# Gated layer of an attention block: PSUM copies of a finished chunk one step later and on ACT alone; scaling of the last weights on ACT, their mean and rests on DVE

## The chip, the cores and the metric

The kernel runs on one core of a Trainium2 chip. The metric is the device time of one execution in microseconds (us). Before the change it is 907.14 us, the median of three runs (907.09, 907.14 and 909.45). Engines are named as in the profile: PE (TensorE matmul), PEld (its weight loads), ACT (ScalarE), DVE (VectorE), POOL (GpSimd) and SP (SyncE, which only issues DMAs here).

## The reference, cut to what matters

Attention with a bias by relative position (4 batches, 8 heads, 576 tokens, heads of 64) gives x with 2304 rows and 512 columns. Then come two layers, all in float32:

```python
# gated layer: x 2304x512; w1, w2 512x1024; w3 1024x1024; w_out 1024x512
a = x @ w1
b = x @ w2
x2 = (a * b @ w3) @ w_out
# last layer: w_in 512x1024, wo2 1024x512, g_ln 1024
h = x2 @ w_in
e = np.exp(h - np.max(h, axis=-1, keepdims=True))
solu = h * e / (np.sum(e, axis=-1, keepdims=True) + 1e-09)
mu = np.mean(solu, axis=-1, keepdims=True)
var = np.mean((solu - mu) ** 2, axis=-1, keepdims=True)
out = (solu - mu) / np.sqrt(var + 1e-06) * g_ln @ wo2
```

The kernel folds `w3 @ w_out` into one matrix on the chip. It scales each row of `wo2` by `g_ln`, and takes the mean over the 1024 scaled rows off each of them, so that `mu` needs no subtraction later.

## The kernel before

**Precision by pairs.** PE multiplies fp32r operands. Each float32 operand is held as a rounded part (hi, an ACT copy) and the rest (lo, a subtraction on DVE or POOL), and each product is three matmuls, hi·hi, hi·lo and lo·hi (`three`, lines 76 to 81). `split` (line 59) makes such a pair: the ACT copy is line 61, the subtraction is line 62, on POOL unless an engine is given.

**Weights arrive as 64-bit words.** They are turned into float32 by a chain of five instructions (`f64_steps`, lines 69 to 73): an absolute value on ACT (line 69), then four on DVE (70 to 73). A conversion is a Python generator (`f64`, line 572). It yields after each instruction, and its last part is `then`, which may give back a `rest` to be run one yield later. A list of waiting conversions is worked off by `convert(n)` (line 607): it steps the two oldest in turn until n yields that did something are counted. A yield of "wait" and the end of a generator count nothing.

**Steps of the gated layer** (`Gated.run`, line 984). The tokens form 6 chunks of 384; with 8 slices of the 1024 middle columns that makes 48 pairs (c, f). Step s issues: the stores of the chunks finished before (`put_outs`); the product a·b of step s-1 (`gate`: ACT copy line 767, DVE product line 768, to HBM by an ACT DMA, line 803); `stage1` of step s (24 matmuls, `ab<-x,ab`); the splits of the slices that are multiplied in this step (`split_g`, lines 61 and 62, `gh` and `gl`); loads of later slices; `convert(3)`, `convert(1)`; `stage2` for one or two slices (12 matmuls each, `x<-gh,wf` and `x<-gl,wf`), which sum over f in one PSUM tile of 4 banks; the sums and splits of a later chunk's input (`next_x`, lines 722, 727 and 729); and `convert(4)`. All engines work in order, so this order of issue decides what stands behind what.

**End of a chunk.** When `stage2` has done f = 7, `x2_out` (line 787) copies the 4 banks to SBUF right there, two on ACT and two on DVE in turn (line 796, tile `x2s`), and the next step stores them. The PSUM tile has one buffer, so the first `stage2` of the next chunk needs it empty.

**Last weights.** After the fold the list holds 8 conversions of `w_in`, 8 of `wo2` (`cv_wo2`, line 886), the mean (`mean_rows`, line 906), 8 last steps of `wo2` (`out_wo2`, line 926), 7 mixtures of `w_in` (`mixed`) and the first input of the last layer. `cv_wo2` scales the tile on POOL (line 895), stores it to `gw_d`, and adds it to `mean` on POOL (lines 898 and 900). `mean_rows` splits `mean`, and after 8 yields multiplies it with a tile of 1/1024 on PE (line 922) and copies the result with ACT (line 923). `out_wo2` loads each scaled tile again, subtracts the mean on DVE (line 934) and splits it with the rest on POOL. The last two of these wait until the last chunk's `stage1` has begun, at step 40.

Of the kernel before, what the change touches and what calls it, by code (L numbers as in the profile page):

```python
# [7 lines left out]
F = mybir.dt.float32  # L8
# [4 lines left out]
ALU = mybir.AluOpType  # L13
# [10 lines left out]
TC = 384  # L24
# [12 lines left out]
class Chip:  # L37


    def __init__(self, tc):  # L40
        self.tc, self.nc = tc, tc.nc
# [478 lines left out]
class Gated:  # L520
# [11 lines left out]
    def __init__(self, ch, i, x_d, x2_d, gw_d, g_d):  # L532
        self.ch, self.nc, self.i = ch, ch.nc, i
        self.x_d, self.x2_d, self.gw_d, self.g_d = x_d, x2_d, gw_d, g_d
        self.left, self.tail, self.right, self.psl, self.psr = (contextlib.ExitStack() for _ in range(5))
        self.M, self.freed = {}, 0
        self.AB, self.W3, self.X, self.XS, self.PS, self.G, self.WF, self.XP = ({} for _ in range(8))
        self.W = [None] * 8
        self.place, self.XC = {}, {}
        self.queue, self.active, self.turn, self.done, self.outs, self.count = [], [], 0, set(), [], 0  # L540
# [246 lines left out]
    def x2_out(self, c):  # L787
        for o in range(0, 4, 2):
            if self.W[0]:
                t = [self.rp.tile([128, 512], F, tag="cm", name="x2s", bufs=6) for _ in range(2)]  # L790
            else:
                t = self.rp.tile([128, 2, 512], F, tag="w3", name="x2s", bufs=3)
                t = [t[:, 0], t[:, 1]]
            for q in range(2):
                copy = self.nc.vector.tensor_copy if q else self.nc.scalar.copy
                copy(t[q][:, :TC], self.XP[c][:, o + q, :TC])
                r = (o + q) * 128
                self.outs.append((self.x2_d[c][r : r + 128], t[q][:, :TC]))

# [86 lines left out]
    def cv_wo2(self, f):  # L886

        nc = self.nc
        if f == 0:
            self.gl = self.pp.tile([128, 8], F, name="gl", tag="gl")  # L890
            self.ch.load(self.gl, self.i["gln"])
            self.mean = self.pp.tile([128, 512], F, name="mean", tag="mean")

        def then(x):
            nc.gpsimd.tensor_scalar(out=x, in0=x, scalar1=self.gl[:, f : f + 1], scalar2=1.0, op0=ALU.mult, op1=ALU.mult)  # L895
            self.ch.load(self.gw_d[f * 128 : f * 128 + 128], x)
            if f == 0:
                nc.gpsimd.tensor_scalar(out=self.mean, in0=x, scalar1=1.0, scalar2=1.0, op0=ALU.mult, op1=ALU.mult)
            else:
                nc.gpsimd.tensor_tensor(out=self.mean, in0=self.mean, in1=x, op=ALU.add)  # L900
            self.done.add(("wo2", f))

        src = self.i["wo2"].bitcast(U)[f * 128 : f * 128 + 128].rearrange("p (a b) -> p a b", a=1)
        return self.f64(src, 1, then, lambda: f == 0 or ("wo2", f - 1) in self.done)

    def mean_rows(self):

        nc = self.nc
        yield
        while not self.done.issuperset([("wo2", n) for n in range(8)]):  # L910
            yield "wait"
        onef = self.rp.tile([128, 512], F, tag="cm", name="onef", bufs=6)
        nc.gpsimd.memset(onef[:, :128], 1.0 / FF)
        ones = self.rp.tile([128, 512], R, tag="cm", name="ones", bufs=6)[:, :128]
        nc.scalar.copy(ones, onef[:, :128])
        t = self.rp.tile([128, 2, 512], R, tag="w3", name="tmp", bufs=3)
        self.ch.split(t[:, 0], t[:, 1], self.mean)
        for _ in range(8):
            yield
        ps = self.aps.tile([128, 2, 512], F, tag="ab", name="ab")[:, 0]  # L920
        for x in range(2):
            nc.tensor.matmul(ps, ones, t[:, x], start=x == 0, stop=x == 1)
        nc.scalar.copy(self.mean, ps)
        self.done.add("mean")

    def out_wo2(self, f):
        yield
        while "mean" not in self.done or (f == 6 and self.last) or (f == 7 and not self.W[6]):
            yield "wait"
        x = self.rp.tile([128, 512], F, tag="cm", name="cm", bufs=6)  # L930
        self.ch.load(x, self.gw_d[f * 128 : f * 128 + 128])
        yield
        yield
        self.nc.vector.tensor_tensor(out=x, in0=x, in1=self.mean, op=ALU.subtract)
        if f < 3:
            t = self.rp.tile([128, 2, 512], R, tag="w3", name="w3", bufs=3)
        elif f < 6:
            t = self.rp.tile([128, 2, 512], R, tag="raw", name="raw", bufs=4)
        elif f == 6:
            self.spare = self.place[0].tile([128, 2, 2, 512], R, tag="ab0", name="ab0")  # L940
        if f > 5:
            t = self.spare[:, f - 6]
        self.ch.split(t[:, 0], t[:, 1], x)
        self.W[f] = t

    def early(self, n):
# [37 lines left out]
    def run(self):  # L984
        steps = [(c, f) for c in range(NC) for f in range(8)]

        order = sorted(steps, key=lambda g: g if g[0] > 1 else (0, g[1] // 2 if g[1] < 2 else g[1], g))
        at = {g: s for s, g in enumerate(order)}
        late = [(self.cv_win, u) for u in range(8)] + [(self.cv_wo2, f) for f in range(8)]
        late += [(self.mean_rows,)] + [(self.out_wo2, f) for f in range(8)]  # L990
        late += [(self.mixed, i) for i in range(7)] + [(self.first_pair,)]
        self.last = True
        plan, n, loaded, used = {}, 0, 0, 0
        for s in range(2 * len(steps)):
            many = 0 if s < self.LAG else 1 if s < self.LAG + 8 else 2
            plan[s] = [g for g in steps[n : n + many] if at[g] < s - self.NEAR]
            n += len(plan[s])
        for s in range(len(self.EARLY), len(steps) + self.NEAR + 1):
            m = s - self.FLAG
            fold = 0 <= m < 8  # L1000
            pace = 4 if s < len(steps) else 2
            now = order[s] if s < len(steps) else None
            self.put_outs()
            for key in list(self.PS):
                self.gate(*key)
            if now:
                self.stage1(*now)
                self.last = now[0] + 1 < NC
                self.freed = 0 if self.last else now[1] + 1
            for g in plan[s]:  # L1010
                self.split_g(*g)
            while s > self.LAG - 3 and loaded < min(used + 4, len(steps)) and at[steps[loaded]] < s - 1:
                self.load_g(*steps[loaded])
                loaded += 1
            used += len(plan[s])
            if fold:
                ps = self.fold(m)
            many = 6 if fold else pace if plan[s] else 7
            self.convert(3)
            self.put_stores()  # L1020
            self.convert(many - 3)
            if fold:
                if now:
                    self.gate(*now)
                self.folded(m, ps)
                self.convert(6)
                if m == 7:
                    self.queue += late
                    self.feed()
            for g in plan[s]:  # L1030
                self.stage2(*g)
                if g[1] == 7:
                    self.x2_out(g[0])
            if now and s > 7 and now[0] + 1 < NC:
                self.next_x(max(2, now[0] + 1), s % 8)
            if plan[s] and not fold:
                self.convert(pace)
        self.put_stores()
        while self.queue or self.active:
            self.convert(1)  # L1040
        self.put_outs()
# [289 lines left out]
```

## Time and profile before

| | |
|---|---|
| median of three runs | 907.14 us |
| the profiled execution's own time | 905.76 us |
| its span, first to last instruction | 904.0 us |
| PE busy | 857.2 us, 95% of the span |
| DVE, ACT, POOL busy | 642.8, 497.0, 348.0 us |
| mean granted TensorE clock | 0.989 |

A span is the time from the first to the last instruction; what lies around it is 1.76 us here. A row of a timeline gives the start, the duration and the engine of an instruction, and in square brackets how long its engine was idle before it and which instruction ended that. The steps that the change touches run from 500 to 692 us; the last layer begins at 692 us.

### The profile page before, as it was taken

Reading aid. Unit: us, or ns where it says so; the run is one execution under the profiler, and the core shown is the slowest. Engines: PE = TensorE matmul, PEld = TensorE weight load, DVE = VectorE, ACT = ScalarE, POOL = GpSimd, SP = SyncE. Lnnn points to the kernel's source line nnn. Section 1 sums busy time; section 2 is a strip of 40 time slices with the busy share of each in tenths; the row PEclk is TensorE's granted clock in tenths of the full one; section 3 lists DMA queues with packets and bytes.
Section 4 is the critical chain, followed back from the end, with each engine's and each line's share of the span. In section 5 each row is a group of like instructions: output and inputs, shape, how many; then the busy total and the mean of one; then the engine's idle time right before and its main releaser. Section 6 shows DMA issues by size and latency. Waiting matters only on the chain.

```text
span 904.0 us, 16035 instructions
## 1 busy us (share of the span) xinstructions
PE 857.2 (95%) x5430; PEld 772.6 (85%) x5430; DVE 642.8 (71%) x1505; ACT 497.0 (55%) x1052; POOL 348.0 (38%) x412
## 2 busy tenths in 40 slices
PE   7979999999999789889999998989999899999998
PEld 3549999999999679878988998989998688888886
DVE  8988989999999789887752677562444855555552
ACT  7978989999999745443322324232334544444432
POOL 3038988888887640000000013340434433323300
PEclk9998999999999999999999999999999999999999
DMA  6897897897985566664523586643234011111001
GB/s 229 295 313 187 232 247 201 256 255 209 294 225 135 190 207 207 240 203 154 190 81 128 180 272 209 221 132 117 70 120 143 1 46 47 48 47 47 24 23 47
DMA packets 93490, 146.31 MB, mean 162 GB/s; under 512 B 11744, under 2 KB 58208, under 8 KB 93408
## 3 DMA queue, kind: packets, MB, share of 16 engines
q1 hardware_dynamic: 86496, 135.85, 49.0%
q10 hardware_dynamic: 6912, 9.44, 2.9%
q8 instruction: 43, 0.70, 0.3%
q14 instruction: 39, 0.32, 0.1%
HBM read 81.93 MB, written 41.30 MB: 136 GB/s over the span
## 4 chain that ended last, share of the span: by engine, by line
PE 72%; DVE 10%; DMA 9%; ACT 3%; issue 3%; POOL 2%; SPq 1%; ACTq 0%; DVEq 0%; POOLq 0%
PE op L446 7%; PE sp L363 6%; PE ab L79 6%; PE ab L80 6%; PE ab L81 6%; PE tp L403 6%; PE o L80 4%; PE o L79 4%; PE o L81 4%; PE ps L191 3%; PE x L80 3%; PE x L81 3%; PE x L79 3%; DMA k<-kr 2%; PE hx L79 2%
## 5 line engine op out<-in xcount | busy, mean ns | idle before, releaser
L79 PE MATMUL ab<-x,ab 128*128 128x384 f32 x320 | 108.4, 339 | 3.0 <-DVE a L768 2.3
L80 PE MATMUL ab<-x,ab 128*128 128x384 f32 x320 | 107.8, 337 | 0.1
L81 PE MATMUL ab<-x,ab 128*128 128x384 f32 x320 | 107.7, 337 | 0.0
L491 DVE TENSOR_TENSOR etl<-tp,eth 128x512 fp32r<-128x512 f32 (+1 forms) x160 | 99.4, 629 | 10.8 <-ACT eth L477 8.4
L393 POOL TENSOR_SCALAR e<-e,st 128x576 f32<-128x576 f32 x128 | 95.1, 754 | 29.8 <-DVE st L389 26.8
L381 ACT ACTIVATE e<-e,st 128x576 f32<-128x576 f32 x128 | 100.2, 783 | 6.0 <-DVE st L374 6.0
L374 DVE CUSTOM_DVE_ANT_0 e<-sp,bt 128x576 f32<-128x576 f32 x128 | 95.5, 747 | 4.1 <-PE sp L363 2.3
L477 ACT CAST eth<-tp 128x512 fp32r<-128x512 f32 (+1 forms) x160 | 85.3, 543 | 18.6 <-PE tp L403 11.9
L403 PE MATMUL tp<-idt,e 128*128 128x128 f32 x576 | 88.0, 276 | 5.5 <-DVE ell L491 3.0
L895 POOL TENSOR_SCALAR cm<-cm,gl 128x512 f32<-128x512 f32 x8 | 6.7, 842 | 219.8 <-DVE cm L73 219.8
L363 PE MATMUL sp<-k,q 128*128 128x288 f32 x256 | 73.5, 302 | 8.6 <-DVE st L374 6.1
L403 PEld LDWEIGHTS tp<-idt,e 128*128 128x128 f32 x576 | 70.2, 142 | 7.7 <-DVE ell L491 3.2
L363 PE MATMUL sp<-k,qz 128*128 128x288 f32 x256 | 72.5, 298 | 0.0
L80 PE MATMUL x<-gl,wf 128*128 128x384 f32 x192 | 65.3, 340 | 5.7 <-DVE gl L62 5.5
L446 PE MATMUL op<-eth,v 128*128 128x288 f32 x256 | 66.0, 339 | 0.4 <-ACT o L479 0.4
L79 PE MATMUL x<-gh,wf 128*128 128x384 f32 x192 | 64.6, 336 | 0.6 <-ACT gh L61 0.6
L81 PE MATMUL x<-gh,wf 128*128 128x384 f32 x192 | 64.5, 336 | 0.0
L79 PEld LDWEIGHTS ab<-x,ab 128*128 128x128 f32 x320 | 60.4, 189 | 4.7 <-DVE a L768 3.7
L80 PEld LDWEIGHTS ab<-x,ab 128*128 128x128 f32 x320 | 60.4, 189 | 0.4 <-DVE x L729 0.4
L1153 POOL TENSOR_TENSOR st<-st,half 128x1 f32<-128x1 f32 x18 | 9.9, 553 | 132.0 <-DVE st L1152 132.0
L81 PEld LDWEIGHTS ab<-x,ab 128*128 128x128 f32 x320 | 60.4, 189 | 0.0
L363 PEld LDWEIGHTS sp<-k,q 128*128 128x128 f32 x256 | 48.8, 191 | 10.6 <-DVE st L374 7.0
(211 smaller groups left out, 2354.3 us busy)
## 6 DMA issues: line engine op xcount, KB each, us to landing
bias_d<-rs SPq DMA_DIRECT2D x36, 295.5 KB, 4.0
qkr<-in_qk SPq DMA_DIRECT2D x16, 640.0 KB, 5.6
k<-kr SPq DMA_DIRECT2D x64, 144.0 KB, 5.7
x_d<-o SPq DMA_DIRECT2D x64, 144.0 KB, 4.2
g_d<-a ACTq DMA_DIRECT2D x48, 192.0 KB, 2.5
gl<-g_d SPq DMA_DIRECT2D x48, 192.0 KB, 2.6
q<-qh SPq DMA_DIRECT2D x64, 128.0 KB, 3.0
raw<-in_wo SPq DMA_DIRECT2D x16, 512.0 KB, 5.0
```

The source lines that it names most:

```text
L79: mm(out, a[0], b[0], start=first, stop=False, skip_group_check=more)
L80: mm(out, a[0], b[1], start=False, stop=False, skip_group_check=more)
L81: mm(out, a[1], b[0], start=False, stop=last, skip_group_check=more)
L191: nc.tensor.matmul(ps[32 * q : 32 * q + 32, x:y], self.cf, m, start=True, stop=True, tile_position=(0, 32 * q))
L363: nc.tensor.matmul(ps[:, half, :HS], w[("q", "qz")[x]][:, h, q * 128 : q * 128 + 128], w["k"][:, h, half * HS : half * HS + HS], start=x = ...
L374: self.nc.vector.tensor_tensor_reduce(out=halves(e), in0=ps[:, :, :HS], in1=halves(self.BT[(self.pairs[n][0], k)]), scale=-0.125, scalar=3e38,
L381: self.nc.scalar.activation(e, e, AF.Exp, bias=st[:, c : c + 1], scale=-1.0, accum_out=st[:, 2 + 2 * c : 3 + 2 * c])
L393: self.nc.gpsimd.tensor_scalar(out=e, in0=e, scalar1=st[:, c : c + 1], scalar2=1.0, op0=ALU.mult, op1=ALU.mult)
L403: tr = lambda c, src: nc.tensor.transpose(ps[: src.shape[1], c * 128 : c * 128 + 128], src, self.idt)
L446: nc.tensor.matmul(w["op"][:, half, :HS], lhs, rhs, start=c == 0 and x == 0, stop=c == 4 and x == 1)
L477: self.nc.scalar.copy(hi, src)
L491: self.nc.vector.tensor_tensor(out=lo, in0=src, in1=hi.bitcast(F), op=ALU.subtract)
```

## The change

Three things change. `x2_out` is no longer called at the end of `stage2`: the chunk is put on a list, `full`, and copied in the next step, behind `gate`, `stage1` and `split_g` and ahead of the loads and conversions (after the last step, behind `put_stores`). All four copies are on ACT. In `cv_wo2` the scaling is an ACT multiplication, the first sum an ACT copy, and the other sums DVE additions, one yield later. In `mean_rows` and `out_wo2` the rests are DVE subtractions, in `out_wo2` one yield later.

```diff
--- before.py
+++ after.py
@@ -533,6 +533,7 @@
         self.ch, self.nc, self.i = ch, ch.nc, i
         self.x_d, self.x2_d, self.gw_d, self.g_d = x_d, x2_d, gw_d, g_d
         self.left, self.tail, self.right, self.psl, self.psr = (contextlib.ExitStack() for _ in range(5))
+        self.full = []
         self.M, self.freed = {}, 0
         self.AB, self.W3, self.X, self.XS, self.PS, self.G, self.WF, self.XP = ({} for _ in range(8))
         self.W = [None] * 8
@@ -792,8 +793,7 @@
                 t = self.rp.tile([128, 2, 512], F, tag="w3", name="x2s", bufs=3)
                 t = [t[:, 0], t[:, 1]]
             for q in range(2):
-                copy = self.nc.vector.tensor_copy if q else self.nc.scalar.copy
-                copy(t[q][:, :TC], self.XP[c][:, o + q, :TC])
+                self.nc.scalar.copy(t[q][:, :TC], self.XP[c][:, o + q, :TC])
                 r = (o + q) * 128
                 self.outs.append((self.x2_d[c][r : r + 128], t[q][:, :TC]))
 
@@ -892,13 +892,18 @@
             self.mean = self.pp.tile([128, 512], F, name="mean", tag="mean")
 
         def then(x):
-            nc.gpsimd.tensor_scalar(out=x, in0=x, scalar1=self.gl[:, f : f + 1], scalar2=1.0, op0=ALU.mult, op1=ALU.mult)
+            nc.scalar.mul(x, x, self.gl[:, f : f + 1])
             self.ch.load(self.gw_d[f * 128 : f * 128 + 128], x)
             if f == 0:
-                nc.gpsimd.tensor_scalar(out=self.mean, in0=x, scalar1=1.0, scalar2=1.0, op0=ALU.mult, op1=ALU.mult)
-            else:
-                nc.gpsimd.tensor_tensor(out=self.mean, in0=self.mean, in1=x, op=ALU.add)
-            self.done.add(("wo2", f))
+                nc.scalar.copy(self.mean, x)
+                self.done.add(("wo2", f))
+                return
+
+            def rest():
+                nc.vector.tensor_tensor(out=self.mean, in0=self.mean, in1=x, op=ALU.add)
+                self.done.add(("wo2", f))
+
+            return rest
 
         src = self.i["wo2"].bitcast(U)[f * 128 : f * 128 + 128].rearrange("p (a b) -> p a b", a=1)
         return self.f64(src, 1, then, lambda: f == 0 or ("wo2", f - 1) in self.done)
@@ -914,7 +919,7 @@
         ones = self.rp.tile([128, 512], R, tag="cm", name="ones", bufs=6)[:, :128]
         nc.scalar.copy(ones, onef[:, :128])
         t = self.rp.tile([128, 2, 512], R, tag="w3", name="tmp", bufs=3)
-        self.ch.split(t[:, 0], t[:, 1], self.mean)
+        self.ch.split(t[:, 0], t[:, 1], self.mean, nc.vector)
         for _ in range(8):
             yield
         ps = self.aps.tile([128, 2, 512], F, tag="ab", name="ab")[:, 0]
@@ -940,7 +945,9 @@
             self.spare = self.place[0].tile([128, 2, 2, 512], R, tag="ab0", name="ab0")
         if f > 5:
             t = self.spare[:, f - 6]
-        self.ch.split(t[:, 0], t[:, 1], x)
+        self.nc.scalar.copy(t[:, 0], x)
+        yield
+        self.nc.vector.tensor_tensor(out=t[:, 1], in0=x, in1=t[:, 0].bitcast(F), op=ALU.subtract)
         self.W[f] = t
 
     def early(self, n):
@@ -1009,6 +1016,8 @@
                 self.freed = 0 if self.last else now[1] + 1
             for g in plan[s]:
                 self.split_g(*g)
+            while self.full:
+                self.x2_out(self.full.pop())
             while s > self.LAG - 3 and loaded < min(used + 4, len(steps)) and at[steps[loaded]] < s - 1:
                 self.load_g(*steps[loaded])
                 loaded += 1
@@ -1030,12 +1039,14 @@
             for g in plan[s]:
                 self.stage2(*g)
                 if g[1] == 7:
-                    self.x2_out(g[0])
+                    self.full.append(g[0])
             if now and s > 7 and now[0] + 1 < NC:
                 self.next_x(max(2, now[0] + 1), s % 8)
             if plan[s] and not fold:
                 self.convert(pace)
         self.put_stores()
+        while self.full:
+            self.x2_out(self.full.pop())
         while self.queue or self.active:
             self.convert(1)
         self.put_outs()
```

## Rows read from the trace of the kernel before

**Rows 1.** Busy time by stretch: PE, PEld, DVE, ACT, POOL, granted clock, DMA share, GB/s

```profile
500.00:692.00 192.00, 185.72 (x1055) 182.81 (x1054) 109.86 (x172) 60.60 (x129) 55.16 (x48) 1.00 0.49 161
538.00:600.00 62.00, 56.98 (x323) 55.68 (x322) 44.10 (x62) 20.91 (x43) 28.43 (x24) 1.00 0.64 205
600.00:632.00 32.00, 31.96 (x184) 31.64 (x183) 8.84 (x18) 6.01 (x14) 0.00 (x0) 1.00 0.35 115
```

**Rows 2.** Waits of PE, 500 to 692 us: total, times, longest

```profile
PE x L80 <- DVE gl L62: 5.5, 6, 2.6
PE x L79 <- ACT gh L61: 0.6, 1, 0.6
```

**Rows 3.** Timeline of PE, the matmuls that waited most

```profile
516.81 0.44 PE L80 MATMUL x<-gl,wf 128*128 128x384 f32 x1 [0.73 <-DVE gl L62]
...
552.10 0.44 PE L80 MATMUL x<-gl,wf 128*128 128x384 f32 x1 [1.66 <-DVE gl L62]
...
561.14 0.44 PE L79 MATMUL x<-gh,wf 128*128 128x384 f32 x1 [0.60 <-ACT gh L61]
561.77 0.44 PE L80 MATMUL x<-gl,wf 128*128 128x384 f32 x1 [0.19 <-DVE gl L62]
...
598.40 0.44 PE L80 MATMUL x<-gl,wf 128*128 128x384 f32 x1 [2.57 <-DVE gl L62]
```

**Rows 4.** Timeline around the end of chunk 1, 545 to 551 us

```profile
545.93 0.34 PE L79 MATMUL ab<-x,ab 128*128 128x384 f32 x1
...
546.13 0.48 ACT L796 COPY x2s<-x 128x384 f32<-128x384 f32 x1 [7.47 <-PE x L81]
...
546.64 0.56 DVE L796 COPY x2s<-x 128x384 f32<-128x384 f32 x1 [6.68 <-ACT x2s L796]
...
547.23 0.48 ACT L796 COPY x2s<-x 128x384 f32<-128x384 f32 x1 [0.62 <-DVE x2s L796]
...
547.61 0.93 ACT L727 CAST x<-xs 128x384 fp32r<-128x384 f32 x2
...
550.10 0.34 PE L79 MATMUL x<-gh,wf 128*128 128x384 f32 x1
```

**Rows 5.** The chain of waits, 540 to 570 us: start, us, what

```profile
547.74 0.56 DVE x2s L796
...
554.42 6.14 DMA gl<-g_d
```

**Rows 6.** The chain of waits, 570 to 605 us

```profile
586.70 6.99 DVE cm L934 x6
593.70 1.13 DVE xs L722
```

**Rows 7.** Groups of DVE, 538 to 600 us: busy us, mean ns, idle before

```profile
L62 DVE TENSOR_TENSOR gl<-gl,gh 128x384 fp32r<-128x384 f32 x14 | 10.6, 798 | 0.2 <-ACT gh L61 0.2
L934 DVE TENSOR_TENSOR cm<-cm,mean 128x512 f32<-128x512 f32 x6 | 7.0, 1232 | 0.0
...
L722 DVE TENSOR_TENSOR xs<-x 128x384 f32<-128x384 f32 x2 | 3.2, 1636 | 0.0
```

**Rows 8.** Groups of POOL, 538 to 640 us

```profile
L900 POOL TENSOR_TENSOR mean<-mean,cm 128x512 f32<-128x512 f32 x7 | 9.8, 1403 | 0.6
...
L62 POOL TENSOR_TENSOR w<-cm,w 128x512 fp32r<-128x512 f32 x3 | 5.0, 1698 | 10.9 <-ACT w L61 10.9
```

**Rows 9.** Line 934, whole span: duration ns least, median, most

```profile
L934 DVE TENSOR_TENSOR cm<-cm,mean x8: 683/693/1781, 586.7 to 632.2; 128x512 f32<-128x512 f32 x8
```

**Rows 10.** Groups of ACT, 500 to 692 us

```profile
L69 ACT ACTIVATE cm<-raw 128x512 f32<-128x512 f32 x8 | 5.4, 671 | 7.5 <-DMA raw<-in_wo 7.5
...
L61 ACT CAST w<-cm 128x512 fp32r<-128x512 f32 x3 | 1.8, 623 | 1.4 <-DVE cm L934 1.4
```

**Rows 11.** Timeline of ACT, two waits that hold what stands behind

```profile
560.58 0.99 ACT L61 CAST gh<-gl 128x384 fp32r<-128x384 f32 x2 [3.24 <-DMA gl<-g_d]
...
579.05 0.59 ACT L923 COPY mean<-ab 128x512 f32<-128x512 f32 x1 [2.03 <-PE ab L922]
```

## The prediction, on record before the run

> **What bounds the kernel now.** I read the busy time by stretch first. From 500 to 692 us, all of the gated layer that the change can reach, PE is busy 185.72 of 192.00 us at a granted clock of 1.00, so PE sets the pace and only its 6.28 idle us can be won [rows 1]. None of the three things changed takes a matmul away or adds one. DVE (109.86 us), ACT (60.60 us) and POOL (55.16 us) are far from full on average [rows 1], so their busy time by itself is worth nothing; what counts is when they deliver.
>
> The waits of PE come next. All 6.1 us of them are for the split of a slice, `gl` or `gh`, at the head of `stage2` [rows 2]. The timeline shows where: 0.73 us at 516.81, 1.66 at 552.10, 0.60 and 0.19 just after 561, 2.57 at 598.40, together 5.75 us [rows 3]. The first three places are the first `stage2` of a chunk, or the step after one.
>
> Then the timeline and the chain around one chunk end say why. ACT had reached the copy of the x2 tile 7.47 us early, stood at it until PE finished, and DVE stood 6.68 us behind it [rows 4]. In these microseconds both could have done the conversions and the next `gate` and splits that are queued behind. They start only when the last copy is over: ACT and DVE take turns, each waiting for the other, from 546.13 to 547.74 + 0.56 = 548.30 [rows 4, 5], 2.17 us. PE needs only 550.10 - 545.93 = 4.17 us for `stage1` [rows 4] and then wants a split that has four conversions, a gate and these copies before it. The 0.79 us after 561 come from the same delay: the load of that `gl` was issued only at 554.42 and took 6.14 us to land [rows 5], and ACT waited 3.24 us for it [rows 11].
>
> The 2.57 us have a second cause. Behind the copies of chunk 2, six subtractions of the mean take 6.99 us in a row [rows 6], 1.232 us each, where the least of that line is 0.683 and the median 0.693 [rows 7, 9]. In the same stretch POOL runs the rests of these tiles at 1.698 us each [rows 8], and the two `xs` sums behind take 1.636 us each [rows 7]. DVE is slowed while POOL works on its own tiles. A sum of 384 columns can't need more than the 0.693 us of 512, so this one queue loses 6 x (1.232 - 0.693) + 2 x (1.636 - 0.693) = 5.1 us.
>
> **The change part by part.**
>
> *The copies, one step later.* Now `gate` and `split_g` of the next step stand before the copies, on ACT and on DVE. What still stands behind the copies is the conversions of that step. Take T as PE's end of the chunk. ACT comes to its four copies before T and waits; then they take 3 x 0.38 + 0.48 = 1.62 us, by the distance of two starts (547.23 to 547.61) and one duration [rows 4]. PE is in `stage1` until T + 4.17, so the PSUM tile is empty 2.55 us before the next chunk's `stage2` wants it. The conversions released at T + 1.62 have until the next `stage2` but one, at T + 4.17 + 4.17 + 4.17 = T + 12.5 (two slices are 24 matmuls, as `stage1` is), for a step's work of DVE, which is 44.10/62.00 of 8.3 us = 5.9 us [rows 1]. It fits by 5 us. The stores of x2 and the loads behind them on SP go out one step later too, but SP no longer stands at a store whose copy waits for PE. So the waits of 0.73, 1.66 and 0.79 us go: 3.18 us. What is late next would be a slice's load, with two steps in hand.
>
> *All copies on ACT.* ACT takes 12 x 0.48 = 5.8 us more, DVE 12 x 0.56 = 6.7 us less [rows 4, 5]. Four in a row on ACT are 0.55 us shorter than the four taken in turn. On this the Trainium skill ("TensorEngine Tiling (Array Packing)", PSUM Bottleneck) says the opposite: use both ScalarE and VectorE to empty PSUM. Two engines side by side would need some 1.04 us by these rows, so ACT alone would be 0.58 us later; but the trace shows turns, not two side by side, and either figure lies under the 4.17 us of `stage1`, so the rule would take something only where ACT comes late, which is the third rival below.
>
> *Scaling and sums of wo2.* POOL loses seven sums of 1.403 us and eight scalings [rows 8]. ACT gets eight scalings and one copy. The trace has no ACT multiplication by a column from SBUF; the nearest rows are an absolute value of the same tile at 0.671 and a cast at 0.623 us [rows 10], and I take 0.67: 8 x 0.67 + 0.62 = 6.0 us on an engine that is busy 20.91 of 62.00 us [rows 1]. DVE gets seven sums at 0.693 us [rows 9], 4.9 us. A new wait comes with it: ACT's scaling waits for DVE's last conversion step, and the `gate` and split copies queue behind it on ACT, for which DVE then waits. That is bounded by zero (DVE has other work at hand) and by 0.67 + 0.48 = 1.15 us a scaling; with 2.4 us free in a step of 8.3 I take zero on PE. SP's store of the scaled tile waits for ACT in place of POOL; same queue, same place.
>
> *Rests of the mean and of out_wo2.* Nine more DVE subtractions at 0.693 us [rows 9], 6.2 us, and nine less on POOL, of 1.698 us each in the first three [rows 8]. In exchange DVE works undisturbed. Over 538 to 632 us: 52.9 us busy now [rows 1], less six copies (3.4), plus fourteen sums and rests (9.7; two rests come after), less 5.1 and at least 14 x (0.798 - 0.693) = 1.5 us of slowing on the splits [rows 7]: 52.6 of 94 us. The 2.57 us wait at 598.40 goes: its queue had 5.1 us of slowing and 2.17 of copies in it and gets up to six rests (4.2) back, spread over more steps.
>
> *More yields.* Eight in `cv_wo2`, eight in `out_wo2`: 16 at 8 a step are two steps, 17 us. Six `out_wo2` would end near 594 + 17 = 611 us instead of at 594 [rows 6]. The last two wait for step 40 anyway, and DVE is busy only 8.84 us of the 32 from 600 to 632 [rows 1]: covered. The matmuls of `mean_rows` move a step too. ACT's copy of their result waits for PE (2.03 us now [rows 11]), and where it falls behind a `stage2` it holds the next gate as the x2 copies did. Bounds: nothing, or another 2.57 us; I take 0.75, near the least chunk-end wait, as only one copy and not four stands there.
>
> *The sum.* 3.18 + 2.57 - 0.75 = 5.0 us off a span of 904.0: 899.0. The profiled execution took 905.76, so 1.76 us around it gives 900.8. The median before, 907.14, is 1.38 above that execution; on its footing the forecast is 902.1 us.
>
> **The rivals.**
>
> 1. *The stall at 598 stays.* DVE, with the rests on it, hands over the splits late, or the mean's copy on ACT takes the place of the x2 copies. For: six subtractions and six rests are 12 x 0.693 = 8.3 us, a whole step. Against: three yields each spread them over more than two steps. Then only the 3.18 us at the chunk ends are won: 907.14 - 3.2 = 903.9.
>
> 2. *The gain is given back.* PE comes earlier, and loads of `gl` (6.14 us once [rows 5]) or the last layer's first splits end last instead. For: the DMA share is 0.64 from 538 to 600 us [rows 1]. Against: it is 0.35 from 600 to 632, where PE is busy 31.96 of 32.00 [rows 1]. Gain near 0.6: 906.5.
>
> 3. *ACT frees the PSUM tile late.* Alone, and behind `gate` and a split that waits for its load (3.24 us [rows 11]), it ends at 3.24 + 1.62 = 4.86, 0.7 us after PE wants the tile, at five chunk ends: 3.5 of the 5.0 us gone, 905.6.
>
> 4. *Slower: ACT and DVE in lockstep.* Each of the eight scalings holds ACT until DVE's step is done and then DVE for 1.15 us, 9.2 us in all, and PE waits it out. It decides once DVE's work in a step is above 8.3 - 1.15 = 7.1 us; it is 5.9 on average, more where two conversions meet. 907.14 - 5.0 + 9.2 = 911.3.
>
> **How the numbers follow.** Forecast 0.64; rivals 0.12, 0.09, 0.06 and 0.09. The forecast's own range is 900.2 (every idle us of PE but 0.3 won, and nothing added: 907.14 - 6.0 = 901.1, and 0.9 for the scatter of runs) to 904.0. To hold 0.8 the range goes on through the first rival and most of the two next: 900.2 to 906.3. A measurement here tells 0.3%, 2.7 us, from no change, so faster means below 904.4: the forecast (0.62 of its 0.64) and most of rival 1 (0.10) give 0.72; no change takes the rest of these and rivals 2 and 3, 0.19; slower 0.09.
>
> **What would show it.** Right: the x2 copies are four on ACT a step after the chunk's end, within 1.7 us, with PE in `ab` matmuls; PE's waits for `gl` from 500 to 692 us add up to about 1 us instead of 6.1; the lines 72, 62, 722 and 934 on DVE keep to one duration up to 630 us; POOL is empty until the mixtures. Wrong: a PE wait of over 1 us behind the mean's copy (rival 1), behind an x2 copy (3), ACT's scaling named as what DVE waits for (4), or the layer ending 5 us earlier with the last layer as much longer (2).

## The result, and the profile after

The changed kernel takes 897.62 us (median of 6 runs, 897.14 to 902.96), the one before 907.12 us in the same comparison. The ratio is 0.9906, with a 95% interval of [0.9885, 0.9927]: 9.5 us faster, 6.6 to 10.4. The forecast was 902.1 us with a range of 900.2 to 906.3. The direction was right, and so was the main mechanism, the place of the copies. The gain is nearly twice the forecast, and the time lies below the range. The profiled execution took 898.74 us, with a span of 897.0. Of the runs further down, one of six of the changed kernel took 1685.01 us, and the median there is that of the other five.

The busy time by stretch answers to [rows 1], with the same columns:

```profile
500.00:692.00 192.00, 191.53 (x1088) 189.07 (x1087) 104.26 (x185) 74.94 (x161) 26.22 (x26) 1.00 0.52 171
538.00:600.00 62.00, 62.00 (x358) 61.90 (x358) 38.23 (x72) 26.48 (x55) 0.21 (x1) 1.00 0.66 218
600.00:632.00 32.00, 32.00 (x186) 32.00 (x185) 9.76 (x18) 9.52 (x21) 0.00 (x0) 1.00 0.32 103
```

PE is never idle from 538 to 632 us. Of the waits in [rows 2] this is all that is left from 500 to 690 us:

```profile
PE x L80 <- DVE gl L62: 0.2, 1, 0.2
```

The end of chunk 1 on the timeline, to be held against [rows 4]:

```profile
545.30 0.34 PE L79 MATMUL ab<-x,ab 128*128 128x384 f32 x1
...
545.50 0.48 ACT L796 COPY x2s<-x 128x384 f32<-128x384 f32 x1 [1.71 <-PE x L81]
...
545.87 1.25 ACT L796 COPY x2s<-x 128x384 f32<-128x384 f32 x3
...
547.55 0.74 ACT L895 ACTIVATE cm<-cm,gl 128x512 f32<-128x512 f32 x1
...
549.46 0.34 PE L79 MATMUL x<-gh,wf 128*128 128x384 f32 x1
```

ACT comes 1.71 us early instead of 7.47. The four copies last from 545.50 to 547.12, 1.62 us as forecast, and PE comes for the tile at 549.46, 2.3 us after it is free. The groups of DVE from 538 to 600 us, for [rows 7], and two groups of ACT from 500 to 692 us:

```profile
L62 DVE TENSOR_TENSOR gl<-gl,gh 128x384 fp32r<-128x384 f32 x14 | 7.1, 549 | 0.0
L903 DVE TENSOR_TENSOR mean<-mean,cm 128x512 f32<-128x512 f32 x7 | 4.8, 685 | 0.1
...
L939 DVE TENSOR_TENSOR cm<-cm,mean 128x512 f32<-128x512 f32 x6 | 4.0, 686 | 0.6 <-DMA cm<-gw_d 0.6
```

```profile
L895 ACT ACTIVATE cm<-cm,gl 128x512 f32<-128x512 f32 x8 | 5.8, 727 | 7.2 <-DVE cm L73 7.2
...
L928 ACT COPY mean<-ab 128x512 f32<-128x512 f32 x1 | 0.6, 589 | 3.1 <-PE ab L927 3.1
```

With POOL empty, DVE's splits fall from 798 to 549 ns and its subtractions of the mean from 1232 to 686. ACT waits 7.2 us for DVE ahead of the eight scalings and 3.1 us for the mean's product, and neither reaches PE.

**How much of it lies in the changed steps.** The matmuls are the same 5430 in both kernels, so PE's own marks can be compared: the first `x` matmul after 503 us, ahead of the first wait that changed, and the first `hx` matmul of the last layer. In the profile of before they start at 503.22 and 691.80, 188.57 us apart; in the one after at 503.60 and 684.77, 181.18 apart. That is 7.39 us, where the idle time of the waits that went is 5.75 [rows 3]. So two questions were open: where the other 1.6 us come from, and where the 2.1 us between this profile and the medians come from. Most experiments below give this distance, called the stretch.

### The profile page after: what moved, and what is told of

Same layout as the page of the kernel before. It is cut to its first block, busy times and chain, and to the rows that moved or that the text cites. A ratio compares the mean times of both kernels' runs of the same rounds, so it can differ in the third digit from the quotient of the medians.

```text
span 897.0 us, 15995 instructions
## 1 busy us (share of the span) xinstructions
PE 855.3 (95%) x5430; PEld 773.3 (86%) x5430; DVE 633.8 (71%) x1509; ACT 506.5 (56%) x1073; POOL 317.6 (35%) x387
## 4 chain that ended last, share of the span: by engine, by line
PE 71%; DVE 8%; DMA 7%; issue 2%; ACT 2%; POOL 2%; SPq 1%; POOLq 0%; ACTq 0%; DVEq 0%
PE op L446 7%; PE ab L80 7%; PE ab L79 7%; PE ab L81 7%; PE sp L363 6%; PE tp L403 6%; PE o L80 4%; PE o L79 4%; PE o L81 4%; PE x L80 3%; PE x L81 3%; PE x L79 3%; DMA k<-kr 2%; PE t L1174 2%; PE hx L79 2%
## 5 line engine op out<-in xcount | busy, mean ns | idle before, releaser
L769 DVE TENSOR_TENSOR a<-ab,a 128x384 f32<-128x384 f32 x48 | 26.6, 554 | 65.5 <-ACT a L768 65.4
```

Of the source, the lines that this page charges most:

```text
L769: nc.vector.tensor_tensor(out=a, in0=ps[:, 1, :TC], in1=a, op=ALU.mult)
```

## The experiments

Each time is of one comparison with the kernel before on the same chip. Theory A: a wait costs PE more than its idle time, about 0.27 us each. Theory B: the rest comes from somewhere else. Theory C came up after the first four runs: the granted clock falls behind some of the waits, and that costs PE more time.

**The changed kernel again.** No edit.

> The changed kernel, once more. Theory A (each wait of PE costs the idle time that the profile gives plus some 0.28 us, since the idle is counted from the modelled end of the matmul before, and the first matmul behind it takes 0.44 us): from the first stage2 after 509 us to the end the kernel is 7.4 us shorter than before, in each execution, and what the medians show beyond that (9.5 us) is scatter of the first 500 us, which the change leaves as they were; the ratio comes near 0.992. Theory B (the waits cost their idle time, 5.75 us, and another 3 to 4 us come from elsewhere, such as DVE no longer slowed by POOL): the ratio stays near 0.9895, and the time from 509 us to the end differs by more than 7.4 us.

Measured: 899.35 us, ratio 0.9918 [0.9891, 0.9945]; the stretch 181.19 us, as in the first profile of the changed kernel to 0.01. The interval holds the ratios of both theories; it is the stretch that speaks for A. The extra cost can be seen in the kernel before, around the wait at 598 us:

```profile
595.50 0.34 PE L79 MATMUL x<-gh,wf 128*128 128x384 f32 x1
598.40 0.44 PE L80 MATMUL x<-gl,wf 128*128 128x384 f32 x1 [2.57 <-DVE gl L62]
598.68 0.34 PE L81 MATMUL x<-gh,wf 128*128 128x384 f32 x1
```

The three starts lie 2.90 and 0.28 us apart, where matmuls back to back start every 0.17 us. So this wait costs 2.84 us, not 2.57.

**Only the copies one step later**, ACT and DVE in turn.

```diff
                 self.split_g(*g)
+            while self.full:
+                self.x2_out(self.full.pop())
...
                 if g[1] == 7:
-                    self.x2_out(g[0])
+                    self.full.append(g[0])
...
```

> Before, with only the copies one step later; ACT and DVE still take turns. Theory A: the waits at the chunk ends go with their 0.28 us each (1.00 + 1.94 + 1.32 + 0.31 = 4.6 us), and the queue of six subtractions at 587 us starts some 1.5 us earlier, so the 2.84 us there shrink to about 1.3: 6.1 us in all, ratio 0.9933. Theory B: 3.2 + 1.3 = 4.5 us, ratio 0.995. If taking turns matters (four copies in 2.17 us, DVE behind ACT), a wait of PE of 0.3 us or more is left at a chunk end.

Measured: 899.23 us, ratio 0.9911 [0.9891, 0.9931]; the stretch 181.69, 6.88 us shorter than in the first profile of before. All that is left of the waits:

```profile
PE x L80 <- DVE gl L62: 0.4, 2, 0.2
```

More than theory A's 6.1: the wait at 598 us goes too, but for 0.12 us. Taking turns leaves no wait at a chunk end.

**Only the copies on ACT alone**, at the old place.

```diff
-                copy = self.nc.vector.tensor_copy if q else self.nc.scalar.copy
-                copy(t[q][:, :TC], self.XP[c][:, o + q, :TC])
+                self.nc.scalar.copy(t[q][:, :TC], self.XP[c][:, o + q, :TC])
```

> Before, with only the copies all on ACT, at the end of the chunk as before. ACT still stands 3.6 to 11 us at the x2 tile, but DVE no longer does. Theory A: if the place of the copies is what counts, the waits at 516, 552 and 561 us stay, each shorter by up to 0.55 us, and the one at 598 stays: 1 to 2 us in all, ratio 0.998 to 0.999. Rival: if DVE's standing behind ACT is what counts, its conversions and sums run on in the 5.5 to 11 us of waiting, and most of the 4.6 us go: ratio 0.995.

Measured: 905.77 us, ratio 0.9989 [0.9974, 1.0005], no change clear of the scatter; the stretch 189.01. The wait at 516 us is gone; those at 552 (1.65 us idle), 561 (1.03) and 598 (2.52) stay. It is the place of the copies that counts, as A said.

**Only the weights' part**: the diff's changes in `cv_wo2`, `mean_rows` and `out_wo2`, with the copies as before.

> Before, with only the scaling, sums and rests of the last weights moved, copies as before. Theory A: the chunk-end waits (4.6 us) stay, and the 2.84 us at 598 go, as DVE is no longer slowed by POOL there: ratio 0.997. Rival (the stall at 598 is a chunk-end wait too, and the rests on DVE take the place of the slowing): a wait of 1 to 2.6 us stays there, ratio 0.999 to 1.000.

Measured: 901.87 us, ratio 0.9939 [0.9916, 0.9963]; the stretch 186.12. The wait at 598 us is gone, and the 0.79 us after 561 with it; those at 516 and 552 stay. This beats both theories, and yet the stretch is 1.6 us longer than its waits explain. The matmul behind the wait at 551 us, and the busy time of two stretches behind it (columns as above, the granted clock third from the end), show why:

```profile
551.11 0.67 PE L80 MATMUL x<-gl,wf 128*128 128x384 f32 x1 [1.96 <-DVE gl L62]
551.58 0.52 PE L81 MATMUL x<-gh,wf 128*128 128x384 f32 x1
```

```profile
551.00:553.00 2.00, 1.90 (x6) 1.90 (x7) 2.00 (x5) 0.00 (x0) 0.00 (x0) 0.54 0.30 107
553.00:555.00 2.00, 2.00 (x9) 2.00 (x8) 0.81 (x3) 1.64 (x4) 0.00 (x0) 0.61 0.55 168
```

Behind 1.96 us of idle the granted clock is near 0.5, the lower of its two levels (1.2 of 2.4 GHz), and a matmul starts every 0.32 us instead of 0.17. The same was to be found behind the wait at 598 us of the kernel with the copies on ACT alone, whose stretch of 189.01 us has 1.6 us of it. Hence theory C.

**Longer waits.** The changed kernel, with ACT's copy of one slice repeated in six steps (13, 16, 16, 20, 20, 22 times, and 19 to 23 in the second kernel).

```diff
         hi, lo = self.G[(c, f)]
+        for _ in range({(1, 2): 13, (1, 6): 16, (2, 2): 16, (2, 6): 20, (3, 2): 20, (3, 6): 22}.get((c, f), 0)):
+            self.nc.scalar.copy(hi, lo.bitcast(F))
```

> The changed kernel, with ACT's copy of one slice repeated (13, 16, 16, 20, 20 and 22 times more) in six steps from 516 to 612 us, so that PE waits for that slice by a length that grows from some 0.4 to 2.4 us; the result is the same. Theory A: each wait costs PE its idle time and 0.27 us, at the full clock. Theory C (the granted clock falls after some waits): behind the longer waits, of about 1.9 us and more, a stretch at a clock near 0.54 takes another 1.5 us, as it did in one wait each of the two kernels with the copies on ACT alone (2.52 us idle) and with the weights' part alone (1.96 us idle).

> The same with 19 to 23 repeats, so that all six waits are 2 to 3 us long. Theory A: 6 x (idle + 0.27). Theory C: the clock falls behind several of the six, each taking 1.5 us more, and not behind every one, since the profile of the kernel before shows 1.66 and 2.57 us of idle with no fall.

Measured, one execution each: 931.14 and 943.14 us. Most waits came out longer than meant: 0.15, 5.93, 2.71, 3.56, 4.09 and 5.44 us in the first kernel, and 3.0 to 6.6 us in the second. Behind the 0.15 us the clock stays. Behind each of the other eleven it falls, and they cost 1.8 to 2.9 us beyond idle and 0.27 us. One of the second kernel, the matmuls and the stretch behind it:

```profile
526.61 0.69 PE L79 MATMUL x<-gh,wf 128*128 128x384 f32 x1 [3.02 <-ACT gh L61]
527.20 0.69 PE L80 MATMUL x<-gl,wf 128*128 128x384 f32 x1
527.69 0.52 PE L81 MATMUL x<-gh,wf 128*128 128x384 f32 x1
```

```profile
527.00:530.00 3.00, 3.00 (x10) 2.80 (x10) 3.00 (x8) 2.31 (x5) 0.00 (x0) 0.50 0.44 94
```

Theory A is too low for these eleven. Theory C holds, with a larger price than the 1.5 us, and the "not behind every one" is a miss: it fell eleven times of eleven.

**The yields alone.** The 16 added yields, with scaling, sums and rests left on POOL.

```diff
-            else:
...
+            def rest():
                 nc.gpsimd.tensor_tensor(out=self.mean, in0=self.mean, in1=x, op=ALU.add)
-            self.done.add(("wo2", f))
+                self.done.add(("wo2", f))
+
+            return rest
...
-        self.ch.split(t[:, 0], t[:, 1], x)
+        self.nc.scalar.copy(t[:, 0], x)
+        yield
+        self.nc.gpsimd.tensor_tensor(out=t[:, 1], in0=x, in1=t[:, 0].bitcast(F), op=ALU.subtract)
```

> Before, with only the 16 added yields: scaling, sums and rests stay on POOL, one yield later as in the changed kernel. If the 2.84 us at 598 us came from DVE being slowed by POOL (theory A), six subtractions still slowed by six rests, some wait of 1 us or more stays there; if they came from six subtractions in one step behind the chunk's end (rival), the spread over two steps takes the wait away with POOL still at work: less than 0.5 us is left. The waits at 516, 552 and 561 us stay in both.

Measured, one execution: 900.46 us, the stretch 184.20. PE's waits from 500 to 690 us, and two groups of DVE from 538 to 600:

```profile
PE x L80 <- DVE gl L62: 2.5, 4, 1.4
```

```profile
L62 DVE TENSOR_TENSOR gl<-gl,gh 128x384 fp32r<-128x384 f32 x14 | 11.9, 887 | 1.0 <-ACT gh L61 1.0
L939 DVE TENSOR_TENSOR cm<-cm,mean 128x512 f32<-128x512 f32 x5 | 5.3, 1125 | 2.5 <-DMA cm<-gw_d 2.5
```

The 0.73 us at 516 and 1.40 at 550 stay, and there is no wait at 598 us; the one after 561 us is gone too, which neither theory had. DVE is as much slowed by POOL as before, 887 ns a split. So the slowing alone does not make the wait at 598 us, and as far as that goes the rival is right: place matters. Five of the six subtractions still stand in a row (5.30 us from 590.54 us, with POOL at work), but a step further from the chunk's end. Two more yields a tile, or the copies out of the way, take the wait away whichever engine makes the rests.

**A version beyond the change.** In the steps that fold weights, the gate is put right behind the fold, ahead of the conversions.

```diff
                 ps = self.fold(m)
+                if now:
+                    self.gate(*now)
...
             if fold:
-                if now:
-                    self.gate(*now)
                 self.folded(m, ps)
```

> The changed kernel, with the gate of a step that folds weights put right behind the fold, ahead of its six conversions. Three waits of PE for a gate (0.57, 0.76 and 0.96 us idle at 426, 462 and 475 us) stand in the kernel before and in the changed one. Theory A with 0.27 us each: they go, 3.1 us, and the time comes to about 0.9965 of the changed kernel, 0.9885 of the one before. Rival: the gate's copy now makes ACT wait for PE ahead of the conversions, whose weights come late for the next fold: a new wait of about the same length, no change.

Measured: 894.84 us against 907.09 (ratio 0.986 [0.9843, 0.9877]); its stretch is 181.21, since the edit lies before it. The busy time from 405 to 500 us of the kernel before, then of this one:

```profile
405.00:500.00 95.00, 92.70 (x470) 83.68 (x469) 54.51 (x107) 29.55 (x56) 0.00 (x0) 1.00 0.42 140
```

```profile
405.00:500.00 95.00, 95.00 (x488) 87.03 (x487) 57.88 (x113) 31.82 (x60) 0.00 (x0) 1.00 0.45 147
```

The three waits are gone, and no wait for a fold came. From 418 us to the mark at 503 us the same matmuls take 81.4 us instead of 84.6 in the changed kernel, 3.2 us less where 3.1 was expected. The ratio lies under the expected 0.9885, which took the change at 7.4 us; with the 8.85 us found below it comes to 0.987, inside the interval. This is the fastest kernel of the study, 12.3 us under the one before.

**Three more profiles of the kernel before**, to see its clock.

> The kernel before, a second profile of it. Its profiled execution took 905.76 us and the medians of its runs are 906.5 to 907.1. Theory C: behind the wait of 2.6 us at 598 us, or that of 1.7 us at 552, the granted clock falls in some executions and not in others, 1.5 us each; an execution of 907 us or more shows such a fall, one of 906 or less shows none, and from PE's step at 503 us to its step at 634 us the kernel takes 130.9 us without a fall and 132.4 with one. Rival: no fall in any, the stretch is 130.9 us each time, and the executions differ in the first 500 us alone.

> The kernel before, a third profile; as for the second: 130.9 us between the two steps without a fall of the clock, 132.4 us with one.

> The kernel before, a fourth profile; as for the second: 130.9 us between the two steps without a fall of the clock, 132.4 us with one.

Measured: 906.76, 904.89 and 907.18 us; the stretch (503 us to `hx`, longer than the two steps named there) 190.19, 190.04 and 189.87 us, where the first profile had 188.57. The wait at 598 us in the first of the three, and its busy time by stretch:

```profile
597.90 0.44 PE L80 MATMUL x<-gl,wf 128*128 128x384 f32 x1 [2.59 <-DVE gl L62]
598.18 0.34 PE L81 MATMUL x<-gh,wf 128*128 128x384 f32 x1
...
599.23 0.53 PE L80 MATMUL x<-gl,wf 128*128 128x384 f32 x1
...
602.34 0.34 PE L81 MATMUL x<-gh,wf 128*128 128x384 f32 x1
```

```profile
598.00:600.00 2.00, 2.00 (x9) 2.00 (x10) 2.00 (x5) 0.54 (x2) 0.00 (x0) 0.70 0.86 267
600.00:602.00 2.00, 2.00 (x8) 2.00 (x7) 0.75 (x2) 0.00 (x0) 0.00 (x0) 0.50 0.44 125
```

and the same stretches in the first profile, on which the forecast rests:

```profile
598.00:600.00 2.00, 1.60 (x9) 1.60 (x10) 2.00 (x5) 1.04 (x3) 0.00 (x0) 1.00 0.93 204
600.00:602.00 2.00, 2.00 (x14) 2.00 (x13) 1.25 (x3) 0.00 (x0) 0.00 (x0) 1.00 0.73 233
```

The clock fell behind this wait in all three, at 1.3 to 1.6 us each. The first profile was the one without a fall. Theory C is right on the price, and wrong that the time of an execution tells: 904.89 us has a fall too. The mark at 503 us lies between 500.97 and 503.39 in the four profiles, a scatter of 2.4 us ahead of the changed steps that hides the 1.5.

**The copies later and on ACT alone**, the weights' part left out: the edits of the second and the third run together.

> Before, with the copies one step later and all on ACT; the weights' scaling, sums and rests stay on POOL. The copies one step later with ACT and DVE in turn took 6.86 us out of the stretch from 509 to 640 us, the whole change 7.37. Theory A: the place of the copies is what counts, so this takes 6.9 to 7.4 us and leaves at most the one wait of 0.12 us at 592; ratio 0.992 to 0.9925. Rival: with ACT alone the DVE queue with its POOL-slowed subtractions gains another 0.5 us and the wait at 592 goes: 7.3 us or more, so that the weights' part of the change brings nothing beside it.

Measured: 898.65 us, ratio 0.9918 [0.9899, 0.9937]; the stretch 181.13 us, where the whole change has 181.18. All that is left of the waits, as in the changed kernel:

```profile
PE x L80 <- DVE gl L62: 0.2, 1, 0.2
```

The rival is right: beside the later copies on ACT the weights' part brings nothing.

## Why the prediction was wrong, step by step

- **What bounds the kernel: right as to place, wrong as to size.** PE's waits for `gl` were what could be won, and they went. But "only its 6.28 idle us can be won" is the sentence that failed, and with it the sum and the low end of the range. Idle time is counted from the modelled end of the matmul before, which runs 0.34 us where the next could start after 0.17; and the one behind the first matmul after a wait starts 0.28 us after it instead of 0.17. From start to start the waits cost 1.00 us (0.73 idle), 1.93 (1.66), 1.33 (0.60 and 0.19) and 2.84 (2.57): 0.27 us more each, in every kernel here, while the clock stays. A matmul at 623.74 us held up PE for 0.31 us with only 0.04 of idle. Together 7.41 us instead of 5.75. In the terms of the sum, 3.18 was 4.57, 2.57 was 2.84, and the 0.75 taken off was nothing: 7.41 in place of 5.0.
- **The clock: not in the prediction.** Behind the wait at 598 us the granted clock fell to its lower level in three of the four profiles of the kernel before, and the forecast rests on the one in which it did not. It took 905.76 us against a median of 907.14, and the step from 900.8 to 902.1 treated these 1.38 us as scatter, to be carried over to the new kernel. Part of it was probably the fall of the clock, which goes with the wait; the timed runs have no profile to show it. On the mean stretch of the other three profiles, 190.03 us, the change gains 190.03 - 181.18 = 8.85 us, within the interval of the ratio.
- **The copies one step later: right.** Timing of the four copies (1.62 us), the free time ahead of PE's need, and the end of the waits at 516, 552 and 561 us are as worked out. Worth 6.88 us alone against the first profile, where 3.18 was forecast, since it also ends the wait at 598 us.
- **All copies on ACT: right, and small.** 181.69 us in turn against 181.13 on ACT alone, 0.56 us. The Trainium skill ("TensorEngine Tiling (Array Packing)", PSUM Bottleneck) says to empty PSUM with both ScalarE and VectorE. The trace does not bear that out for two engines that take turns: they need 2.17 us [rows 4, 5], ACT alone needs 1.62. What two engines side by side would need, no run here shows.
- **The second cause of the wait at 598: not enough by itself.** DVE is slowed by POOL as described, but with the slowing left in and only the yields or only the place of the copies changed, the wait goes. Whether the wait would also go with the slowing alone taken away, no run shows; the 5.1 us that the prediction worked out for it are more than the wait, so it may well have been needed for it too. That the 2.57 us term held for the whole change was in part luck: the later copies alone end this wait, which the prediction gave to the weights' part. It was worth 2.84 us, or 4.1 to 4.4 where the clock fell.
- **Scaling on ACT: right on time, 0.727 us for the 0.67 taken.** ACT waits 7.2 us for DVE ahead of it, and the slower rival (lockstep) did not come: there was room.
- **The 0.75 us for the mean's copy: wrong.** The copy waited 3.1 us for PE, and what stood behind it still came in time for PE.
- **The rivals.** None of the four is seen. In the changed kernel PE waits behind no x2 copy, no scaling and no load; and the last layer, from the first `hx` matmul to the end, is as long as before (212.2 us to the last instruction in both profiles), so nothing was given back. The wait that the copies or the weights' part could have left at 598 us is gone by either of them alone, so their gains do not add: 6.88 us and 2.45 us alone (a fall of the clock is in the second), 7.39 together.

Not settled: the medians give gains of 9.5 and 7.1 us for the changed kernel in two comparisons, and of 8.2 us for the copies later and on ACT alone. That this spread is the scatter of the first 500 us fits the marks, but the timed runs themselves have no profile to show it.

## What to carry to other kernels

Price a wait of TensorE from the start of one matmul to the start of the next, not by its idle time, and ask for the granted clock behind it in several profiles before calling one execution typical. An instruction that waits for the end of a long product belongs behind everything on its queue that the next product needs; moving it took six lines and was worth 6.88 us of the 7.39, and with all copies on ACT the whole. When two edits each end the same wait, run each alone before crediting either.

## What the runs showed of the hardware

The granted clock behind a wait was not the same from one execution to the next. Between 500 and 690 us, waits with 1.40 to 1.67 us of idle were followed by the full clock each time (six in six profiles). One of 1.96 us was followed by half the clock. Of five with 2.52 to 2.59 us four were, and all eleven from 2.71 us on. What it costs, with the waits of 1.96 to 2.59 us, is 1.3 to 1.6 us beyond the wait; with the longer ones it is 1.8 to 2.9. The length of the wait alone does not decide: at 382.9 us, ahead of the changed steps, 2.47 us of idle were followed by the full clock in the first profile of the kernel before, and 1.82 us in that of the changed kernel by a granted clock of 0.62 and then 0.53.
